# A gated linear-attention layer and its feed-forward layer: all token chunks in pairs of two batches, with the small matrix products on 64x64 parts of the array

## Chip, core and metric

The kernel runs on one core of a Trainium2 chip. The metric is the device time of one execution in microseconds (us). Five engines run their own instruction streams and wait for each other through semaphores: TensorE (PE; its weight loads are listed apart as PEld), VectorE (DVE), ScalarE (ACT), GpSimd (POOL) and SyncE (SP), which here issues nearly all DMA transfers. SBUF is the on-chip memory, PSUM the eight-bank memory that TensorE writes its products to.

## The reference

Four batches, eight heads, 768 tokens, 48 numbers per head. A state of 48x48 per batch and head decays by `w` and takes up one outer product per token; the output `y` of a token reads the state, and its own outer product with a bonus weight `u`. The outputs of the eight heads (384 numbers) then pass through two dense layers with a leaky ReLU between them.

```
for t in range(S):                      # S = 768; r, k, v, w: [4, 8, 768, 48]
    cur = einsum('bhd,bhe->bhde', u * k[t], v[t])
    y[t] = einsum('bhd,bhde->bhe', r[t], state + cur)
    state = w[t][..., None] * state + einsum('bhd,bhe->bhde', k[t], v[t])
x = y.transpose(0, 2, 1, 3).reshape(3072, 384)
h = x @ w_in                            # 384 -> 2048
out = maximum(0.01 * h, h) @ w_out      # 2048 -> 384
```

## The kernel before

**Chunks.** The recurrence is cut into chunks of 128 tokens, 6 per batch, 24 in all (numbered `n` in the order in which they are worked on, `seq`). Inside a chunk, the running sums of log w make decayed copies of r and k, and y comes from three products: masked scores (r times k) with v, the carried state with r, and the bonus. The next state is the decayed state plus k times v. One chunk uses, per engine:

- SP: a load each of w, k, r, v (line 701 for single chunks).
- ACT: log of w (711), the exponentials (743, 747) and the decay of the whole chunk, `a` (738).
- TensorE: running sums of log w by a triangular matrix (717) and the chunk totals against a column of ones (720); transposes of r and k (416); scores (858); new sums for the state, k times v (798); carried state with r (824); masked scores with v (829); transposes of y (464).
- DVE: the exponents' sums (729), products with r and k (405), masks on the scores (788), bonus reduction (443), new state (813), y plus bonus (478).
- POOL: bonus products (435, 439, 447), cast of v (455), decayed state (775).

**Two forms.** `pair` (483 to 685) works on two consecutive chunks of one batch, two tokens to a partition; it serves the first two chunks of batches 0 and 1, n = 0 to 3, with the state handed from the first to the second chunk inside it (592 to 612). Its scores (624) run on 64x64 parts of the array and its masked products (649) and state sums (583) on 64x128 parts; the bonus is added by TensorE (`add_vs`, 668) and y is only copied (678, 680). `single` (687 to 845) works on one chunk, one token to a partition, for n = 4 to 23; in seven cases (`MERGED`) the scores of two singles are issued together by `run`.

**Transposes by DMA.** For the chunks in `RK_DMA` the transposes of r and k, and for those in `Y_DMA` the transposes of y, are made by DMA transfers that SP issues (764, 843); for the others by TensorE.

**Dense layers.** `blocks` of one or two chunks: the first matrix product (901, "up") fills a PSUM bank, ACT applies the leaky ReLU (916), the second product (928, "down") sums over 16 pieces, DVE or ACT copies the result (939, 941), SP stores it (945). Weights are loaded in pieces through the buffers `in` and cast to bf16 (335 to 361).

**Order.** Nothing is ordered by hand: `Plan` (23 to 152) lists all steps with engines, assumed costs, priorities and buffers, runs an event simulation, and the instructions are then issued in the order that this gave, on every engine in order. `RANK` (162) adds offsets to the priorities of the first 144 steps and `FORCE` (179) fixes the engine of some. Each PSUM use takes one of eight banks `ps`, with limits per kind (319). `LEAD` and `AHEAD` say how far log w and the loads may run ahead. Until 24 us, gaps of TensorE in the plan are filled with products of zeros (970).

Of the kernel before, what the change touches and what calls it, by code (L numbers as in the profile page):

```python
# [15 lines left out]
class Buf:  # L16


    def __init__(self, pool, kind=None):
        self.pool, self.kind, self.users, self.t, self.free_at = pool, kind or pool, [], None, 0.0  # L20


class Plan:
# [7 lines left out]
    def __init__(self, limits, slack_from, slack, late):  # L31
        self.steps, self.limits, self.late = [], limits, late
        self.slack_from, self.slack = slack_from, slack
# [8 lines left out]
    def order(self, pools):  # L42
# [10 lines left out]
        remain = {k: len(b.users) for k, b in bufs.items()}  # L53
        free_tiles = {p: [(0.0, k) for k in range(len(t))] for p, t in pools.items()}
        in_use = {}
        ready_at = [0.0] * n
        self.start, self.done, self.eng = [None] * n, [0.0] * n, [None] * n
# [15 lines left out]
        while events:  # L73
# [13 lines left out]
            for e in self.ENGINES:  # L87
# [3 lines left out]
                while ready[e]:  # L91
# [3 lines left out]
                    want, ok = {}, True  # L95
                    for b in self.steps[i][5]:
                        if b.t is None:
                            want[b.pool] = want.get(b.pool, 0) + 1
                            if in_use.get(b.kind, 0) >= self.limits.get(b.kind, 99):
                                ok = False  # L100
                    for p, k in want.items():
                        if sum(f <= now + 1e-9 for f, _ in free_tiles[p]) < k:
                            ok = False
# [10 lines left out]
                for b in takes:  # L114
                    if b.t is None:
                        slots = free_tiles[b.pool]
                        s = min(slots)
                        slots.remove(s)
                        b.slot = s[1]
                        b.t = pools[b.pool][s[1]]  # L120
                        in_use[b.kind] = in_use.get(b.kind, 0) + 1
                d = engs[e]
                self.start[i], self.eng[i] = now, e
# [7 lines left out]
                else:  # L131
# [5 lines left out]
                    self.done[i] = dma_free + lat + (self.late if now > 20 else 0.0)  # L137
                heapq.heappush(events, (free[e], 1, e, -1))
# [5 lines left out]
                for b in {id(b): b for b in (*reads, *takes)}.values():  # L144
                    b.free_at = max(b.free_at, self.done[i])
                    remain[id(b)] -= sum(u == i for u in b.users)
                    if remain[id(b)] == 0:
                        free_tiles[b.pool].append((b.free_at, b.slot))
# [7 lines left out]
BOTH = (1.5, 64, 1.45, 0.2)  # L156
WEIGHT = (2.08, 24, 2.6, 0.2)
# [4 lines left out]
RANK = {0: 15.37, 1: 14.4, 2: 3.33, 3: 23.03, 4: 38.76, 5: 12.01, 6: -26.8, 7: -21.87, 8: -21.96, 9: -19.05,  # L162
# [22 lines left out]
def kernel(  # L185
# [91 lines left out]
    with tc.manual_schedule():  # L277
# [10 lines left out]
        for t in pools["lw"]:  # L288
            nc.vector.memset(t[:, :, D:64], 0.0)
# [715 lines left out]
```

## Time and profile before

| | |
|---|---|
| three runs | 181.78, 182.65, 183.76 us; median 182.65 |
| the profiled execution | 181.38 us, its span 179.6 us |
| granted TensorE clock | 0.996 |
| up products (L901), 720 | 73.3 us busy |
| down products (L928), 384 | 73.4 us busy |
| leaky ReLU (L916, ACT), 96 | 56.8 us busy, 597 ns each |
| masks on single chunks' scores (L788, DVE), 40 | 25.1 us busy, 683 ns each |
| bonus products (L435, L439, POOL), 24 each | 1001 and 1027 ns each |
| loads of single chunks, 80 | 192 KB each, 4.0 to 4.2 us from issue to landing |
| transposes by DMA | 13 of r and k (3.9 us to landing), 8 of y (3.7) |
| moved by DMA | 34.43 MB in 116571 packets, 109121 of them under 512 B |

Times in the profile are counted from the start of the span. A group's busy time merges overlapping instructions of an engine: durations of matrix products overlap, so the distance from one start to the next is what a product takes from TensorE. The chain that ended last follows the work back from the last instruction, each time to what released it. A stretch table gives the busy time of each engine between two times.

### The profile page before, as it was taken

The page shows a single profiled execution, that of the slowest core. Times are in us where ns is not written, and L with a number is a line of the kernel's source. Part 1 is how long each engine was busy: PE and PEld are TensorE (multiplying, and loading weights), DVE is VectorE, ACT ScalarE, POOL GpSimd, SP SyncE. Part 2 cuts the span into 40 slices and gives each one's busy share as a digit, 9 for nine tenths or more (in the row PEclk, how much of TensorE's full clock was granted, in tenths as well). Part 3 has the DMA queues.
Part 4 walks back from the last instruction along what each step waited for, and adds up shares of the span by engine and source line. Part 5 has one row for each costly group of instructions (what it writes and reads, how often), then busy time and mean ns, then how long its engine had stood idle before and what let it go on. Part 6 is the DMA issues. An engine that isn't in the chain of part 4 may idle for free.

```text
span 179.6 us, 5197 instructions
## 1 busy us (share of the span) xinstructions
PE 171.6 (96%) x2036; PEld 129.8 (72%) x2037; DVE 115.0 (64%) x231; ACT 115.3 (64%) x253; POOL 102.5 (57%) x138
## 2 busy tenths in 40 slices
PE   7798999999999999999999999999999999999991
PEld 2466888867778788877788767787788786787850
DVE  7699764289789898559677558397468297241102
ACT  2678968855867788884489774485486664652610
POOL 5999632574897686877469854667165665100000
PEclk9999999999999999999999999999999999999998
DMA  5999999998999999999999989999899996600112
GB/s 141 261 283 316 370 376 364 187 199 199 231 191 224 180 229 134 184 213 173 185 181 223 212 179 223 153 215 175 152 254 170 220 163 134 167 9 19 47 44 88
DMA packets 116571, 34.43 MB, mean 192 GB/s; under 512 B 109121, under 2 KB 115778, under 8 KB 116546
## 3 DMA queue, kind: packets, MB, share of 16 engines
q1 hardware_dynamic: 116544, 34.09, 95.8%
q8 instruction: 16, 0.26, 0.7%
q14 instruction: 9, 0.07, 0.1%
q10 hardware_dynamic: 2, 0.00, 0.0%
HBM read 25.17 MB, written 4.72 MB: 166 GB/s over the span
## 4 chain that ended last, share of the span: by engine, by line
PE 77%; DMA 11%; DVE 4%; ACT 2%; issue 2%; SPq 1%; POOL 0%; DVEq 0%; ACTq 0%
PE ps L901 35%; PE ps L928 28%; DMA in<-in_r_dram 3%; DMA in<-in_v_dram 3%; DMA in<-in_w_dram 2%; PE ps L858 2%; DMA xT<-y 2%; PE ps L829 2%; PE ps L717 2%; PE ps L824 2%; PE ps L416 2%; DVE rk L405 2%; PE ps L798 1%; PE ps L464 1%; DVE m L636 1%
## 5 line engine op out<-in xcount | busy, mean ns | idle before, releaser
L901 PE MATMUL ps<-xT,w_in_b 128*128 128x256 bf16 (+1 forms) x720 | 73.3, 251 | 0.4 <-ACT xT L471 0.2
L928 PE MATMUL ps<-w_out_b,g 128*128 128x384 bf16 x384 | 73.4, 326 | 0.0
L916 ACT ACTIVATE g<-ps 128x512 bf16<-128x512 f32 x96 | 56.8, 597 | 25.4 <-PE ps L901 23.2
L901 PEld LDWEIGHTS <-w_in_b 128*128 128x128 bf16 x720 | 57.8, 98 | 9.9 <-issue 0.7
L928 PEld LDWEIGHTS <-g 128*128 128x128 bf16 x384 | 35.2, 98 | 17.3
L405 DVE TENSOR_TENSOR rk<-in,ps 128x384 bf16<-128x384 f32 x46 | 24.5, 548 | 9.9 <-ACT ps L743 6.5
L435 POOL TENSOR_TENSOR ru<-in,ub 128x384 f32<-128x384 f32 x24 | 23.9, 1001 | 9.6 <-DMA in<-in_k_dram 7.6
L788 DVE TENSOR_TENSOR m<-ps,maskb 128x512 bf16<-128x512 f32 x40 | 25.1, 683 | 5.3 <-PE ps L858 5.3
L439 POOL TENSOR_TENSOR ru<-ru,in 128x384 f32<-128x384 f32 x24 | 24.6, 1027 | 3.0 <-DMA in<-in_r_dram 2.4
L775 POOL TENSOR_TENSOR sb<-s,a 128x384 bf16<-128x384 f32 x18 | 15.0, 831 | 16.8 <-ACT a L738 16.8
L447 POOL TENSOR_TENSOR vs<-in,dg 128x384 f32<-128x384 f32 x20 | 16.6, 830 | 9.1 <-DVE dg L443 8.4
L729 DVE TENSOR_TENSOR ci<-ps,lw 128x384 f32<-128x384 f32 x20 | 11.1, 555 | 9.7 <-PE ps L720 4.5
L939 DVE COPY o<-ps 128x384 f32<-128x384 f32 x10 | 5.6, 555 | 15.6 <-PE ps L928 15.4
L443 DVE TENSOR_REDUCE dg<-ru 128x8 f32<-128x384 f32 x24 | 12.9, 544 | 2.1 <-POOL ru L439 2.1
L478 DVE TENSOR_TENSOR y<-ps,vs 128x384 bf16<-128x384 f32 x20 | 11.1, 553 | 3.2 <-PE ps L829 2.6
L455 POOL CAST vb<-in 128x384 bf16<-128x384 f32 x24 | 12.0, 504 | 1.5 <-DMA in<-in_v_dram 1.4
L711 ACT ACTIVATE lw<-in 128x384 bf16<-128x384 f32 x20 | 10.4, 522 | 2.9 <-DMA in<-in_w_dram 2.9
L743 ACT ACTIVATE ps<-ps 128x384 f32<-128x384 f32 x20 | 9.6, 481 | 4.1 <-DVE ci L729 3.6
L738 ACT ACTIVATE a<-ps 64x4 f32<-64x4 f32 x36 | 6.0, 167 | 7.7 <-DVE ci L729 5.1
L813 DVE TENSOR_TENSOR s<-ps,sb 128x384 f32<-128x384 f32 x14 | 7.7, 552 | 3.8 <-PE ps L798 2.7
L747 ACT ACTIVATE ps<-ci 128x384 f32<-128x384 f32 x20 | 9.8, 491 | 0.0
L941 ACT COPY o<-ps 128x384 f32<-128x384 f32 x14 | 6.7, 479 | 4.2 <-PE ps L928 4.0
(90 smaller groups left out, 176.2 us busy)
## 6 DMA issues: line engine op xcount, KB each, us to landing
out_dram<-o SPq DMA_DIRECT2D x24, 192.0 KB, 3.7
in<-in_w_dram SPq DMA_DIRECT2D x20, 192.0 KB, 4.2
in<-in_k_dram SPq DMA_DIRECT2D x20, 192.0 KB, 4.2
in<-in_r_dram SPq DMA_DIRECT2D x20, 192.0 KB, 4.0
in<-in_v_dram SPq DMA_DIRECT2D x20, 192.0 KB, 4.0
in<-in_moe_w_out_dram SPq DMA_DIRECT2D x4, 768.0 KB, 12.1
in<-in_moe_w_in_dram SPq DMA_DIRECT2D x4, 384.0 KB, 6.8
in<-in_moe_w_in_dram SPq DMA_DIRECT2D x2, 768.0 KB, 9.0
```

Of the source, the lines that this page charges most:

```text
L405: (nc.gpsimd if e == "POOL" else nc.vector).tensor_tensor(out=o, in0=x, in1=i, op=ALU.mult)
L435: lambda e: nc.gpsimd.tensor_tensor(out=ru.t[:], in0=kv(), in1=ubv, op=ALU.mult),
L439: lambda e: nc.gpsimd.tensor_tensor(out=ru.t[:], in0=ru.t[:], in1=rv(), op=ALU.mult),
L443: lambda e: nc.vector.tensor_reduce(out=dg.t[:], in_=ru.t[:], axis=AX.X, op=ALU.add),
L447: lambda e: nc.gpsimd.tensor_tensor(out=vs.t[:], in0=vv(), in1=dg.t[:].unsqueeze(2).to_broadcast([128, H, D]), op=ALU.mult),
L455: {"POOL": 0.56}, lambda e: nc.gpsimd.tensor_copy(out=vb.t[:], in_=vv()),
L478: lambda e: nc.vector.tensor_tensor(out=y.t[:], in0=heads(yp.t), in1=vs.t[:], op=ALU.add),
L775: lambda e: nc.gpsimd.tensor_tensor(out=sb.t[:].rearrange("p g a d -> p (g a) d"), in0=s_in.t[:].rearrange("p g a d -> p (g a) d"), in1=a_ ...
L788: lambda e, par=par: nc.vector.tensor_tensor(out=m.t[:, par, :, :], in0=sc[par].t[:].rearrange("p (g t) -> p g t", g=NP), in1=maskb[:].uns ...
L901: nc.tensor.matmul(hp.t[:, a * N : (a + 1) * N], lhsT=w_in_b[:, t, (j + a) * 128 : (j + a + 1) * 128], rhs=xT[:, t, c0 : c0 + N], start=(a ...
L916: lambda e, hp=hp, g=g, j=j, J=J, N=N: nc.scalar.activation(out=g.t[:, j : j + J, 0:N], in_=hp.t[:, 0 : J * N].rearrange("p (a n) -> p a n ...
L928: nc.tensor.matmul(op.t[:, 0:DM], lhsT=g.t[:, j, off : off + 128], rhs=w_out_b[:, j, :], start=(j == 0), stop=(j == NJ - 1))
```

## The change

Everything works in pairs now, and a pair is the same chunk of two neighbouring batches: batch 0 on partitions 0 to 63, batch 1 on 64 to 127, with two tokens to a partition. `seq` is chunk by chunk over all four batches.

- `pair` (n = 0 and 2) makes the first chunks of batches 0, 1 and 2, 3. There is no state yet, so the chunk totals, the decayed state, its product with r and the identity product that added it are gone. The state sums run on 64x64 parts.
- `late` (n = 4, 6, ... 22) takes the place of `single` and `run`. Running sums come from two products and eight small ones for the totals of both batches. The small products all run on 64x64 parts of the array, with the row part and the PSUM bank tied together, in two steps: scores with half of the carried-state products; then the other half, masked scores with v, and state sums.
- The loads are one transfer per tensor and batch, 64 partitions each, with pieces of 384 bytes in place of 192. `in` is one tile of 33 slots that are taken two or four at a time, where it was ten of four.
- The tokens of a late pair stay in the order (first tokens of all partitions, then second); the leaky ReLU reads its PSUM bank in that order and writes the natural one.
- Transposes by DMA: all pairs from n = 8 on, two chunks per transfer, both for r and k and for y. Before, 13 chunks for r and k and 8 for y.
- The last chunk's down product, copy and store are cut into columns 0 to 255 and 256 to 383.
- `blocks` becomes [2, 2, 1, 1, 2, ...]; `LEAD` 6, `AHEAD` 20; `RANK` and `FORCE` are empty. The plan now takes neighbouring slots, keeps a bank from being used by TensorE and another engine at once, and doubles TensorE's costs before 6.5 us.
- At the start: eight small selects on POOL for a new mask `maskp`, one for `maskb` and three memsets less; on DVE memsets of `u_row` and of two more `rk` tiles.

The core of the diff:

```diff
-RANK = {0: 15.37, 1: 14.4, 2: 3.33, 3: 23.03, 4: 38.76, 5: 12.01, 6: -26.8, 7: -21.87, 8: -21.96, 9: -19.05,
...
-FORCE = {23: "DVE", 26: "DVE", 29: "ACT", 30: "DVE", 46: "ACT", 58: "ACT", 61: "ACT", 79: "ACT", 85: "DVE",
...
+RANK = {}
+FORCE = {}
...
-    RK_DMA = {6, 11, 12, 14, 15, 16, 17, 18, 19, 20, 21, 22, 23}
-    Y_DMA = {8, 10, 16, 17, 20, 21, 22, 23}
-    MERGED = {6, 10, 12, 14, 16, 18, 20}
-    LEAD = 4
-    AHEAD = 4
+    RK_DMA = {8, 10, 12, 14, 16, 18, 20, 22}
+    Y_DMA = {8, 10, 12, 14, 16, 18, 20, 22}
+    LIMITS = {"hp": 2, "op": 2, "cp": 1, "ek": 3, "yy": 2, "warm": 1, "warm2": 1}
+    LAST = [(0, 256), (256, DM)]
+    LEAD = 6
+    AHEAD = 20
-    blocks = [2, 1, 1, 1, 1, 2, 2, 2, 2, 2, 1, 1, 2, 2, 2]
+    blocks = [2, 2, 1, 1, 2, 2, 2, 2, 2, 2, 2, 2, 2]
+    seq = [(b, c) for c in range(C) for b in range(B)]
...
+        def late(n):
...
+                for x in range(2):
+                    def load(e, src=src, name=name, x=x):
+                        nc.sync.dma_start(
+                            out=Flat(slots[name]).t.rearrange("p (h f) -> p h f", h=H)[64 * x : 64 * x + 64],
+                            in_=src[b + x, :, t0 : t0 + L, :].rearrange("h (p j) d -> p h (j d)", j=2))
...
+            def scores(e):
+                for js in range(2):
+                    for g in range(NP):
+                        for par in range(2):
+                            q0 = 64 * par
+                            for x in range(2):
+                                q = slice(64 * x, 64 * x + 64)
+                                nc.tensor.matmul(
+                                    scs[js][par].t[q, g * 128 : (g + 1) * 128].rearrange("p (j t) -> p j t", j=2),
+                                    lhsT=rkT2.t[q0 : q0 + D, js, NP + g, q], rhs=rkT2.t[q0 : q0 + D, :, g, q],
+                                    start=True, stop=True, skip_group_check=True)
+            def sums(e):
+                for g in range(NP):
+                    for js in range(2):
+                        for x in range(len(pps)):
+                            q = slice(64 * x, 64 * x + 64)
+                            for par in range(2):
+                                nc.tensor.matmul(
+                                    pps[x].t[64 * par : 64 * par + 64, g * D : (g + 1) * D],
+                                    lhsT=rk2.t[q, js, 1, 2 * g + par, :], rhs=vbs[js].t[q, 2 * g + par, :],
+                                    start=(g == 0 and js == 0), stop=(js == 1), skip_group_check=True)
+            def inter(flip):
+                def go(e):
+                    for g in range(NP):
+                        for x in range(2):
+                            par = x ^ flip
+                            q0, h = 64 * par, 2 * g + par
+                            for j in range(2):
+                                summed(x, j, slice(h * D, (h + 1) * D), lhsT=rkT2.t[q0 : q0 + D, j, g, 64 * x : 64 * x + 64],
+                                       rhs=sbs[x].t[q0 : q0 + D, g, :])
+                return go
+            def intra(e):
+                for h in range(H):
+                    for js in range(2):
+                        for x in range(2):
+                            q = slice(64 * x, 64 * x + 64)
+                            for j in range(2):
+                                summed(x, j, slice(h * D, (h + 1) * D), lhsT=ms[js].t[q, h % 2, h // 2, 64 * j : 64 * j + 64],
+                                       rhs=vbs[js].t[q, h, :])
...
+            s_sc = step(
+                {"PE": 0.75}, row(inter(1), scores), P0 + 1, deps=[*s_T, *s_sbs], reads=[rkT2, *sbs],
+                takes=[sc for js in range(2) for sc in scs[js]] + yps)
...
+            s_yi = step(
+                {"PE": 0.7 if last else 0.9}, row(inter(0), intra, *([] if last else [sums])), P0 + 2,
+                deps=[*s_ms, *s_vbs, *s_T, *s_sbs, s_rk[1, 0], s_rk[1, 1]], reads=[*ms, *vbs, rk2, rkT2, *sbs],
+                takes=[*yps, *pps])
...
+                def leaky(e, hp=hp, g=g, j=j, J=J, N=N, c0=c0):
+                    o, i = g.t[:, j : j + J, 0:N], hp.t[:, 0 : J * N]
+                    if c0 < B:
+                        i = i.rearrange("p (a n) -> p a n", a=J)
+                    else:
+                        i = i.rearrange("p (a x t) -> p a t x", x=2, t=64) if N == L else i.rearrange("p (s x t) -> p s t x", x=2, t=64)
+                        o = o.rearrange("p a (t x) -> p a t x", x=2) if N == L else o.rearrange("p a (s t x) -> p (a s) t x", x=2, t=64)
+                    nc.scalar.activation(out=o, in_=i, func=AF.Prelu, alpha=0.01)
```

`summed` is a product that adds to `yps[x]` on the partitions of token half `j`; `row` issues its parts one after the other as one step.

More of the change, by code (lines that the diff above doesn't have):

```diff
@@ L753, in single @@
[L753 to L762 removed]
+                        heads(c1.t), lhsT=mat[:], rhs=lw.t[:, j, :, 0:D], start=(j == 0), stop=(j == 1),
@@ new lines, in late @@
+            s_cg = step(
+                {"DVE": 0.55},
+                lambda e: nc.vector.tensor_tensor(out=cg.t[:], in0=heads(c1.t), in1=lw.t[:, 1, :, 0:D], op=ALU.add),
+                P0, deps=[s_cum], reads=[c1, lw], takes=[cg])
+            ek0, ek1, er0 = (Buf("ps", "ek") for _ in range(3))
+            s_k0 = step(
+                {"ACT": 0.5}, lambda e: nc.scalar.activation(out=heads(ek0.t), in_=heads(c1.t), func=AF.Exp, scale=-1.0),
+                P0, deps=[s_cum], reads=[c1], takes=[ek0])
@@ new lines, in late @@
+            s_yi = step(
+                {"PE": 0.7 if last else 0.9}, row(inter(0), intra, *([] if last else [sums])), P0 + 2,
+                deps=[*s_ms, *s_vbs, *s_T, *s_sbs, s_rk[1, 0], s_rk[1, 1]], reads=[*ms, *vbs, rk2, rkT2, *sbs],
+                takes=[*yps, *pps])
+            for x in range(0 if last else 2):
+                sx = Buf("s")
+                prev[b + x] = (sx, [step(
+                    {"DVE": 0.35},
+                    lambda e, x=x, sx=sx: nc.vector.tensor_tensor(
+                        out=sx.t[:], in0=part(pps[x].t), in1=sbs[x].t[:], op=ALU.add),
+                    P0 + 2, deps=[s_yi], reads=[pps[x], sbs[x]], takes=[sx])])
```

875 lines of the change are left out of this document (449 added, 426 removed), and 16 rows, old and new, of the table RANK.

## Prediction

> **What bounds the kernel now.** I read the page first, then busy time by stretch, the chain that ended last, and TensorE's timeline. The page's busy line:
>
> ```profile
> PE 171.6 (96%) x2036; PEld 129.8 (72%) x2037; DVE 115.0 (64%) x231; ACT 115.3 (64%) x253; POOL 102.5 (57%) x138
> DMA  5999999998999999999999989999899996600112
> ```
>
> TensorE leads, but DMA engines read 9 as well, so stretches have to decide (columns: stretch, length, then busy us and count of PE, PEld, DVE, ACT, POOL; clock; DMA share; GB/s):
>
> ```profile
> 19.00:36.00 17.00, 16.77 (x234) 14.15 (x234) 8.61 (x14) 13.38 (x24) 7.99 (x10) 1.00 1.05 321
> 89.00:120.00 31.00, 31.00 (x343) 24.18 (x342) 21.14 (x41) 21.44 (x51) 20.31 (x25) 1.00 1.20 197
> 150.00:176.00 26.00, 25.91 (x221) 18.64 (x220) 6.76 (x13) 10.98 (x20) 2.76 (x4) 1.00 0.24 59
> ```
>
> From 19.0 us (the chain's first L901) to 176.0 TensorE is never without work for more than a few tenths, at full clock. DMA at 1.2 never starves it. So the span is a front of 19.0, 157.0 of TensorE work, and a tail of 3.6 (176.0 to 179.6). Only less TensorE work, an earlier first L901 or a shorter tail can help; any new gap costs in full.
>
> Prices on TensorE come from start-to-start distances, since durations overlap (start, duration, instruction, count):
>
> ```profile
> 60.03 0.33 PE L717 MATMUL ps<-lw,trev 128*128 128x384 bf16 x1
> 60.19 0.24 PE L720 MATMUL ps<-ones,lw 128*128 128x1 bf16 x4
> 60.29 0.33 PE L464 MATMUL ps<-ident,y 128*128 128x128 bf16 x3
> 60.46 0.33 PE L798 MATMUL ps<-vb,rk 128*128 128x96 bf16 x4
> 60.72 0.40 PE L858 MATMUL ps<-rkT 48*128 48x128 bf16 x8
> 61.05 0.82 PE L928 MATMUL ps<-w_out_b,g 128*128 128x384 bf16 x4
> ...
> 64.04 0.33 PE L824 MATMUL ps<-sb,rkT 128*128 128x96 bf16 x4
> 64.21 0.36 PE L829 MATMUL ps<-vb,m 128*128 128x48 bf16 x8
> 64.42 0.61 PE L416 MATMUL ps<-ident,rk 128*128 128x128 bf16 x8
> 64.86 0.33 PE L798 MATMUL ps<-vb,rk 128*128 128x96 bf16 x4
> 65.03 0.33 PE L717 MATMUL ps<-lw,trev 128*128 128x384 bf16 x1
> ```
>
> Decay sums: 0.16 for 384 columns, 0.10 for the four totals. Transposes: y 0.17, r and k 0.44. Sums (L798) 0.17, but 0.26 ahead of L858: 0.09 to enter the split array. Scores of one chunk 0.33; the chain has sixteen of two chunks in 0.55, so eight cost 0.22 and 0.11 is for leaving. A visit to a split array thus costs 0.20 beside its products. Carried state (L824) 0.17, masked product (L829) 0.21.
>
> For small parts there are only the first pairs:
>
> ```profile
> 10.86 0.64 PE L624 MATMUL ps<-rkT 48*64 48x128 bf16 x32
> L624 PE MATMUL ps<-rkT x64: 213/216/240, 10.9 to 18.7; 48*64 48x128 bf16 x64
> L649 PE MATMUL ps<-vb,m x64: 179/179/193, 14.3 to 22.1; 64*128 64x48 bf16 x64
> ```
>
> On four 64x64 parts (L624), 32 products take 0.64 with one duration of 0.216, so (0.64-0.216)/31 = 13.7 ns each: four in 55 ns. L649, on two row parts with 48 columns, runs 32 in 0.57 (14.33 to 14.90): 12.6 each, two in 25 ns. The longest durations are those that waited for a weight load: 240-213 = 27 ns for 64 columns on four parts, 193-179 = 14 on two.
>
> **The change, part by part.** *Late pairs on TensorE (the largest term).* Before, 20 single chunks: decay 20x0.16 + 72/4x0.10 = 5.0; scores 7 merged x(0.55+0.09) + 6 x(0.33+0.09) = 7.0; sums 16x0.17 = 2.7; carried state 18x0.17 = 3.1; masked 20x0.21 = 4.2; transposes on TensorE 7x0.44 + 12x0.17 = 5.1. Sum 27.1. After, ten pairs: decay 0.32+0.20 = 0.52 each, 5.2. First visit: 32 scores x13.7 ns + 16 carried-state products + 0.20; second: 16 + 64 masked + 32 sums (none in the last two pairs) + 0.20. The 48-column product on four parts is nowhere in the trace: between 6.3 ns (four in the 25 ns that a part takes) and 12.6 (four no better than two). I take 7: a part's period is then the 27 ns weight load, which the records show running under the previous product. Visits: 0.75 and 0.98 (0.76 in the last two), so 7.5+9.4 = 16.9. Transposes stay for chunks 4 to 7: 4x(0.44+0.17) = 2.4. Sum 24.5: **-2.6**. There are 1,216 such products, so each ns is 1.2 us: -3.4 to +4.2.
>
> [...]
>
> *Rest of TensorE.* First pair 2 after 19.0 loses the carried-state product and identity add (L656, L601): 4x0.04+0.16, -0.3. Of 288 up-projections with 128 columns, 192 become 96 with 256: 192x0.0556-96x0.109, -0.2. Splitting the last output's columns adds nothing that shows.
>
> *Tail, -0.5.* The last copy is 128 columns for 384: L939's 0.555 less 256 at 1.0 ns (slope from L788: 512 columns 0.683) saves 0.25. The store carries a third; of its 3.0 us (176.56 to the end) I take 0.25.
>
> *Front, -0.5 (bounds -1.5 and +1.0).* First pair 0 loses the state steps that lie between its masks and y (sb 0.47 among them on the chain). Against it: eight more selects on POOL at 0.2 to 0.3 (L306's 0.29 is the nearest), minus one and three memsets, and about 0.8 of DVE memsets; POOL's first bonus product stands at 6.28 directly behind the selects, and `add_vs` needs its results. Loads are the same bytes in two issues each; they wait in SP's queue behind the transfers either way.
>
> *Other engines, nothing.* Per two chunks DVE changes from 9.3 to about 9.0 (state 192 columns), ACT loses about 0.7, POOL gains two half-height products of 0.83 less two halved sb, some +0.8, so 111 of 179. SP: loads 88 to 96, transposes 21 to 16 (double size); late loads move 384-byte pieces, as in the first pairs' slices (261 to 283 GB/s against some 200 later), which covers larger transposes. All lie under TensorE, with 30% free; gone that cover, ACT comes next. The leaky step reads PSUM in alternating halves: no row has that; bounds 0 and the 0.15 by which strided L423 copies differ (0.59 to 0.74); I take 0, off the path.
>
> *New waits, +1.0 (0 to 5).* Pair 4's chunks come as one: w of chunk 4 was issued at 23.5 and TensorE met its y only at 42.4. Twice the loads (1.57 MB, 6 us at 261 GB/s) lie ahead while pairs 0 and 2 last until about 19+21+4: 0.5. The scores take four score banks and two y banks in one step, of eight, and the 144 hand ranks are gone: 0.05 a pair, 0.5. Behind each such wait stand the up and down products, on an engine that runs in order.
>
> Sum: -2.6-0.3-0.2-0.5-0.5+1.0 = -3.1. Span 176.5; with 1.8 around it 178.3 against 181.4. The median of the runs shown is 182.65, so **179.5**.
>
> **Rivals.** *A: four parts do no better than two,* since each part waits for its weights or its instructions. Place: the second visit, 224 instructions with the weight loads against 96 in the densest stretch now (L583 and L649). For it: no 48-column row on four parts, no run so long. Against: the 27 ns. Price 1,216x5.6 ns = +6.8: 186.3, slower. It decides from 9.5 ns a product, where the gain is gone. [...]
>
> *B: TensorE waits in each pair.* Six banks at once need both output kinds nearly drained, and masks hold them for up to 4x0.68. For it: the order is new, and today's has under 1 us of gaps, so it can only get worse. Against: DVE, ACT and POOL are at 57 to 64%. At 0.5 us for ten pairs: 184; at 0.3 no gain is left.
>
> *C: only the cover changes.* The cheaper products are real but the later pair 4 and front eat them (+2.5): 182, no change.
>
> **How the numbers follow.** Forecast 0.48, A 0.18, B 0.19, C 0.15. One per cent, about what a measurement of this kernel can tell, is 180.8 to 184.5. The forecast lies faster in nine cases of ten (0.43), some of C too (0.02); same: the rest of the forecast (0.05), most of C (0.12) and a quarter of B (0.05), 0.22; slower: A, most of B (0.14) and a hundredth of C, 0.33. Range: product at 6.3, front at -1.5 and no waits give 176.6; upper end A's 186.5.
>
> **What would show it.** Right: a 48-column product on 64x64 parts at 7 ns start to start, visits of 0.75 and 1.0, TensorE without gaps from some 18.5 to 172.5. Wrong: 12 ns (A), gaps before scores (B) or before pair 4's first up product (C), or ACT above 600 ns in the leaky step.

## The result: 12% slower, and the profile after

The changed kernel takes 204.63 us (median of four runs, 203.46 to 206.38) against 183.08 for the kernel before (181.78 to 183.76): ratio 1.119, interval [1.108, 1.131]. The forecast was 179.5 with a range up to 186.5: wrong in sign, and outside the range. One run of the experiment with the first pairs' loads at full height, 1.9% above the fastest of its kernel, is left out of its time below.

The changed kernel's profiled execution took 205.48 us, its span 203.8 us. From its page: the busy line, DMA by fortieths of the span, and the queue q8, which brings instructions in packets of 16 KB (packets, MB, share):

```profile
PE 178.5 (88%) x3001; PEld 129.8 (64%) x3004; DVE 111.8 (55%) x234; ACT 103.5 (51%) x201; POOL 115.1 (57%) x165
...
DMA  5999999999999999799999999999999923111112
...
q8 instruction: 23, 0.38, 0.8%
```

TensorE falls from 96% to 88%, with no other engine above 57%, while the DMA engines read 9 nearly throughout, up to the last fifth. The same three stretches as before, changed kernel:

```profile
19.00:36.00 17.00, 15.34 (x203) 11.32 (x204) 9.88 (x17) 9.67 (x18) 7.82 (x10) 0.90 1.10 313
89.00:120.00 31.00, 28.18 (x643) 21.12 (x631) 19.90 (x39) 16.01 (x33) 25.71 (x34) 1.00 1.12 196
150.00:176.00 26.00, 24.41 (x423) 18.17 (x424) 12.47 (x23) 11.17 (x21) 7.44 (x11) 1.00 0.69 117
```

Before, TensorE was busy in all but 0.3 us of these stretches; now it is idle for 1.7, 2.8 and 1.6. What ended its idle time, from the changed kernel's table of waits (line waited, releaser: us, times, longest):

```profile
PE ps L757 <- ACT lw L744: 5.8, 5, 3.3
PE ps L874 <- DMA rkT<-rk: 2.2, 1, 2.2
PE ps L874 <- issue: 2.0, 1, 2.0
...
PE ps L874 <- DVE rk L446: 1.5, 3, 0.8
PE ps L762 <- issue: 1.4, 1, 1.4
...
PE ps L990 <- issue: 1.2, 1, 1.2
...
PE ps L868 <- issue: 0.9, 1, 0.9
```

There are two families. One is late data: running sums (L757) that wait for the log of w (L744), which itself waited for loads of w for 12.9 us, and the carried-state products (L874) that open the step of the scores and wait for a transpose by DMA. The other is "issue", where TensorE waits for nothing that a semaphore shows. One such stop lies inside a second visit to the split array (timeline of TensorE, changed kernel):

```profile
80.88 0.39 PE L874 MATMUL ps<-vb,m 64*64 64x48 bf16 x28
83.27 0.47 PE L874 MATMUL ps<-vb,m 64*64 64x48 bf16 x36 [2.00 <-issue]
83.56 0.44 PE L868 MATMUL ps<-vb,rk 64*64 64x48 bf16 x32
```

Counted in TensorE's instruction stream, the four stops under "issue" after the first up product (5.5 us) fall at numbers 1982, 2238, 3262 and 4286. All leave the rest 190 by 256. The packets of q8 have 16384 bytes, 23 of them for some 6,000 instructions of TensorE, so a packet is taken here as a page of 256 instructions, and each of these stops is at the border of one.

And the front. From 2 to 10 us only the first pairs' loads run, the same bytes in the same 384-byte pieces. The same stretch before, then after (last column GB/s):

```profile
2.00:10.00 8.00, 6.79 (x52) 3.57 (x52) 6.17 (x22) 4.27 (x9) 7.35 (x17) 1.00 1.19 258
```

```profile
2.00:10.00 8.00, 7.28 (x30) 3.46 (x29) 5.73 (x25) 3.86 (x6) 7.35 (x21) 1.00 1.15 199
```

The DMA engines are as busy as before and move a quarter less. In the packet records, a 384-byte piece takes 28.0 ns on average before and 35.2 after. What differs is the transfer: 384 KB to 128 partitions in one, or 192 KB to 64.

The span in four terms, from the starts and ends of matrix products (the row of the forecast is the kernel before with the prediction's terms added; the last three kernels are experiments below):

| us | first up | gaps on TensorE after it | its work after it | tail | span |
|---|---|---|---|---|---|
| before | 19.0 | 0.8 | 156.2 | 3.7 | 179.6 |
| changed | 22.5 | 17.0 | 161.3 | 3.0 | 203.8 |
| forecast | 18.5 | 1.8 | 153.1 | 3.2 | 176.5 |
| first pairs' loads at full height | 19.8 | 15.5 | 161.1 | 3.0 | 199.4 |
| all loads at full height | 19.8 | 3.4 | 157.8 | 3.0 | 184.0 |
| the same, wide masked products | 19.8 | 1.5 | 157.0 | 3.0 | 181.4 |

### The profile page after: what moved, and what is told of

The parts are those of the page before. It is cut to its first block, busy times and chain, and to the rows that moved or that the text cites. A ratio compares the mean times of both kernels' runs of the same rounds, so it can differ in the third digit from the quotient of the medians.

```text
span 203.8 us, 7137 instructions
## 1 busy us (share of the span) xinstructions
PE 178.5 (88%) x3001; PEld 129.8 (64%) x3004; DVE 111.8 (55%) x234; ACT 103.5 (51%) x201; POOL 115.1 (57%) x165
## 4 chain that ended last, share of the span: by engine, by line
PE 41%; DMA 28%; SPq 10%; POOL 9%; issue 5%; DVE 3%; ACT 3%; POOLq 0%; ACTq 0%; DVEq 0%
PE ps L1021 18%; PE ps L990 16%; DMA in<-in_w_dram 12%; DMA in<-in_v_dram 6%; SPq L538 6%; DMA in<-in_r_dram 4%; DMA rkT<-rk 4%; PE ps L874 3%; POOL vs L841 2%; POOL ru L831 2%; SPq L731 2%; DMA out_dram<-o 2%; POOL ru L827 1%; ACT lw L744 1%; PE ps L857 1%
## 5 line engine op out<-in xcount | busy, mean ns | idle before, releaser
L1021 PE MATMUL ps<-w_out_b,g 128*128 128x384 bf16 (+2 forms) x400 | 76.8, 322 | 1.0 <-DVE w_out_b L401 1.0
L841 POOL TENSOR_TENSOR vs<-in,dg 64x384 f32<-64x384 f32 x40 | 33.0, 825 | 3.7 <-DVE dg L835 1.6
L926 DVE TENSOR_TENSOR m<-ps,maskp 128x512 bf16<-128x512 f32 x40 | 24.9, 682 | 11.1 <-PE ps L857 11.1
L827 POOL TENSOR_TENSOR ru<-in,ub 128x384 f32<-128x384 f32 x20 | 19.8, 1000 | 8.4 <-DMA in<-in_k_dram 8.4
L1032 DVE COPY o<-ps 128x384 f32<-128x384 f32 (+1 forms) x14 | 7.5, 537 | 30.1 <-ACT g L1010 18.7
L744 ACT ACTIVATE lw<-in 128x768 bf16<-128x768 f32 x10 | 8.4, 842 | 14.3 <-DMA in<-in_w_dram 12.9
L914 POOL TENSOR_TENSOR sb<-s,a 128x192 bf16<-128x192 f32 x20 | 9.8, 508 | 8.6 <-ACT ps L786 4.7
L835 DVE TENSOR_REDUCE dg<-ru 128x8 f32<-128x384 f32 x20 | 10.8, 548 | 3.3 <-POOL ru L831 3.2
L1066 PE MATMUL ps<-zeros 128*128 128x128 bf16 (+1 forms) x38 | 9.3, 357 | 2.0 <-DVE zeros L319 1.7
L874 PEld LDWEIGHTS <-rkT 48*64 48x64 bf16 x320 | 4.6, 107 | 10.0 <-issue 5.3
L874 PE MATMUL ps<-sb,rkT 48*64 48x48 bf16 x320 | 7.1, 192 | 4.0 <-DMA rkT<-rk 2.2
L1034 ACT COPY o<-ps 128x384 f32<-128x384 f32 (+1 forms) x11 | 5.2, 473 | 9.0 <-PE ps L1021 8.7
L777 DVE TENSOR_TENSOR ci<-ps,lw 128x384 f32<-128x384 f32 x10 | 5.5, 555 | 7.5 <-PE ps L762 2.9
```

The lines of the kernel that those rows point to most:

```text
L827: lambda e, ru=ru, j=j: nc.gpsimd.tensor_tensor(out=ru.t[:], in0=view("k", j)(), in1=ubv, op=ALU.mult),
L835: lambda e, ru=ru, dg=dg: nc.vector.tensor_reduce(out=dg.t[:], in_=ru.t[:], axis=AX.X, op=ALU.add),
L841: lambda e, x=x, j=j, q=q, dg=dg: nc.gpsimd.tensor_tensor(out=vs2[x].t[64 * j : 64 * j + 64], in0=view("v", j)()[q], in1=dg.t[q].unsqueeze ...
L874: nc.tensor.matmul(yps[x].t[64 * j : 64 * j + 64, cols], start=(x, j) not in begun, stop=True, skip_group_check=True, **k)
L926: lambda e, par=par, js=js: nc.vector.tensor_tensor(out=ms[js].t[:, par, :, :], in0=scs[js][par].t[:].rearrange("p (g t) -> p g t", g=NP), ...
L1021: nc.tensor.matmul(op.t[:, d0:d1], lhsT=g.t[:, j, off : off + 128], rhs=w_out_b[:, j, d0:d1], start=(j == 0), stop=(j == NJ - 1))
```

## Experiments

The theory after the result had two parts: loads of half height (to 64 partitions) are slow and make everything behind them late (L), and dense small products run out of instructions (P). Against it stood an order that is worse without its ranks (O), the larger transposes (X), and four parts that are no better than two (A). Ratios are to the kernel before, which was run beside each experiment (medians 181.6 to 181.8 us); the changed kernel was not run again, so differences to its 204.6 us can be off by 1 to 2 us.

**The kernel before with loads of half height.** Every load of r, k, v, w is cut into two of 64 partitions:

```diff
-                    nc.sync.dma_start(out=part(i)(), in_=src[b, :, t0 : t0 + L, :].rearrange("h p d -> p h d"))
+                    for x in (0, 64):
+                        nc.sync.dma_start(
+                            out=part(i)()[x : x + 64], in_=src[b, :, t0 + x : t0 + x + 64, :].rearrange("h p d -> p h d"))
```

(and the first pairs' loads likewise.) 

> The kernel before with every load cut into two transfers of 64 partitions each; same bytes, same pieces, same order. Theory L (transfers of half height are slow, and the changed kernel's late start and its waits for w come from them): between 2 and 10 us the DMA engines move about 200 GB/s in place of 258, the first up product starts at 21 to 23 us in place of 19.0, and the time rises by 4 to 15 us. Theory P (the loss is in the supply of TensorE's instructions) and theory O (the loss is the order without hand ranks): rate, first up product and time stay within 1 us, near 183.

Measured 219.15 us, ratio 1.205 [1.199, 1.211]. From 2 to 10 us it moves 200 GB/s where the kernel before moves 258, and the first up product comes at 24.2: the changed kernel's slow front comes without the rest of the change, and comes out larger (L had 21 to 23). The time, 37 us more, is far beyond L's 4 to 15, for what follows is not a clean copy: 36 to 60 us have only 145 GB/s at a DMA share of 0.72, and the chain has 18.8% of the span in SP issuing the single chunks' loads, which are now twice as many. So this run speaks for the front alone.

**The changed kernel with two queues for the halves.** The second batch's loads of pairs 0 and 2 are issued by ACT.

```diff
-                            nc.sync.dma_start(
+                            (nc.scalar if b else nc.sync).dma_start(
...
-                            {"SP": 0.55}, load, P0 + "wkrv".index(name) * 0.1 + 0.5 * x, takes=[slots[name]],
+                            {"ACT" if b else "SP": 0.55}, load, P0 + "wkrv".index(name) * 0.1 + 0.5 * x, takes=[slots[name]],
```

> The changed kernel with the second batch's loads of the first two pairs (8 of 96 transfers) issued from ScalarE's queue, so that both halves of the partitions are being filled at once. Theory L: 2 to 10 us moves 250 GB/s or more in place of 199, the first up product starts at 19 to 20 in place of 22.5, w of chunk 4 is seen 2 to 4 us earlier, and the time falls by 3 to 7 us to 198 to 201. If the rate is set by the pieces or the memory and not by the height: 199 GB/s again and 204 to 206.

Measured 205.78, ratio 1.132 [1.125, 1.138]; 199 GB/s from 2 to 10 us and the first up product at 22.7, as without the edit, although 4,226 packets (1.57 MB) now come by ACT's queue and alternate with SP's from 4 us on. The queue is not the reason. This is also a miss of L as it was put: L had 250 GB/s or more once both halves are filled at once, and 199 is what the other side foretold. What decides between them are the loads alone and the kernels with loads at full height, below.

**The kernel before without its ranks.**

```diff
-RANK = {0: 15.37, 1: 14.4, 2: 3.33, 3: 23.03, 4: 38.76, 5: 12.01, 6: -26.8, 7: -21.87, 8: -21.96, 9: -19.05,
...
+RANK = {}
+FORCE = {}
```

> The kernel before with empty rank and engine tables, nothing else. Theory O: 8 us or more slower than before, with gaps on TensorE of several us. Theories L and P: at most 3 us slower, TensorE's gaps after the first up product under 3 us in all.

Measured 182.97, ratio 1.006 [1.004, 1.009]: the hand-made order was worth 1.1 us in the kernel before, far from 22.

**Small products alone.** A long run of 48-column products on four 64x64 parts, then bursts of 112 between full products.

```diff
+        burst(768)
+        full(24)
+        for _ in range(6):
+            burst(112)
+            full(24)
```

> Only TensorE products (none of the computation): 768 products of 48 columns on four 64x64 parts in one run, then six bursts of 112 between 24 products of 256 columns on the full array, then twelve such bursts while 64 loads of half height run. Theory P (instructions come in pages of 256, and a dense burst outruns the next page): in the long run 6.3 to 7.5 ns a product inside a page and a stop of 0.5 to 2 us at nearly every 256th instruction; in the bursts without loads fewer or shorter stops, with loads stops of 1 to 2 us at page borders that fall in or shortly behind a burst. If the supply is a steady rate: one even distance between products, above 7 ns, with no stop at any border.

The long run (timeline of TensorE):

```profile
14.31 1.62 PE L32 MATMUL small<-a 64*64 64x48 bf16 x175
18.33 1.23 PE L32 MATMUL small<-a 64*64 64x48 bf16 x128 [2.40 <-issue]
21.79 1.91 PE L32 MATMUL small<-a 64*64 64x48 bf16 x128 [2.23 <-issue]
25.24 1.91 PE L32 MATMUL small<-a 64*64 64x48 bf16 x128 [1.55 <-issue]
```

128 products with their 128 weight loads are 256 instructions, one page. At full clock (the second line) they take 1.04 us, start to start of the first and last, 8.2 ns a product; then TensorE stops until the next page has come, and pages arrive every 3.45 us. No load runs in this stretch (5 GB/s from 18.3 to 33.3 us), so the supply alone is the limit: 13.5 ns an instruction when sustained. The six bursts with full products between them have two such stops (0.4 and 0.7 us); with half-height loads running, the same bursts stop at nearly every border, 0.3 to 1.8 us each. (From some 20 us on, in the midst of the stops, the clock is 0.5; the mean from 18.3 to 33.3 us is 0.56.)

**Loads alone, by shape.** Eight stretches of loads, each begun after the one before has landed; the first two, in which `whole` is a transfer to 128 partitions and `half` one to 64:

```diff
+        for i in range(8):
+            whole(i, i)
+        between()
+        for i in range(16):
+            half(i // 2, 8 + i // 2, i % 2, i % 2)
+        between()
```

> Leaves out all of the computation: only loads, in eight stretches of some 3.1 MB, each begun after the one before has landed (the seventh has 1.6 MB). 1: 8 transfers of 128 partitions, 8 heads, 384-byte pieces. 2: 16 transfers of 64 partitions, lower and upper half in turn. 3: 16 transfers of 64 partitions, lower half alone. 4: 16 transfers of 128 partitions, 4 heads each, so as large as those of 2. 5: 16 transfers of 128 partitions with 192-byte pieces. 6: as 2, lower halves from SP's queue and upper ones from ACT's. 7: 32 transfers of one head for both batches (128 partitions, 384-byte pieces, 49 KB), from two queues. 8: as 1. Theory L (a transfer that reaches only 64 partitions is slow by its height, whatever the number, the size or the queue of the transfers): 1, 4 and 8 reach 250 to 290 GB/s; 2 and 6 stay at some 200, and 3 at 200 or less. Rival S (small transfers are slow, by their size or number): 4 falls to 200 as 2 does, and 7 far below. Rival H (halves are filled one after the other, one half at a time): 6 returns to 250 or more, 3 is slower than 2. Stretch 5 gives the price of the 192-byte pieces that the kernel before used later on: some 200 by the rates of the later stretches there, if those were bound by transfers at all.

The middles of the eight stretches (last two columns: DMA share, GB/s):

```profile
6.00:12.00 6.00, 5.24 (x8) 0.00 (x0) 1.00 1.17 325
24.00:34.00 10.00, 1.52 (x6) 0.00 (x0) 1.00 1.21 223
43.00:53.00 10.00, 2.54 (x10) 0.00 (x0) 1.00 1.32 207
60.00:68.00 8.00, 1.52 (x6) 0.00 (x0) 1.00 1.07 290
77.00:87.00 10.00, 1.52 (x6) 0.00 (x0) 1.00 1.15 222
97.00:105.00 8.00, 1.41 (x6) 0.00 (x0) 1.00 1.28 246
120.00:150.00 30.00, 0.51 (x2) 0.00 (x0) 1.00 0.15 40
159.00:165.00 6.00, 1.27 (x5) 0.00 (x0) 1.00 1.17 325
```

Full height reaches 325 in the first and the last stretch. Half height, halves in turn: 223; lower half alone: 207; halves from two queues: 246. Full height in transfers as small as the halves: 290, so the size and number of the changed kernel's transfers account for a small part at most. 192-byte pieces at full height: 222, what 384-byte pieces reach at half height, so the doubled pieces of the change gained nothing. Over the whole stretches the packet records have 22.3, 30.9, 36.2, 23.1, 15.7 and 30.2 ns a piece in 1 to 6. Stretch 7 is slow as S has it (40 GB/s), but at a DMA share of 0.15, with pieces of 22.1 ns: there the engines mostly stand idle, which is a different limit from the changed kernel's. Theory L holds for transfers of 192 KB, at higher rates than it gave; S falls for them; H gets a little: filling both halves at once gives 8 to 19%, not the 40 to 57% that are missing.

**Masked products on 64x128 parts.**

```diff
-                            for j in range(2):
-                                summed(x, j, slice(h * D, (h + 1) * D), lhsT=ms[js].t[q, h % 2, h // 2, 64 * j : 64 * j + 64],
-                                       rhs=vbs[js].t[q, h, :])
+                            nc.tensor.matmul(
+                                yps[x].t[:, h * D : (h + 1) * D], lhsT=ms[js].t[q, h % 2, h // 2, :], rhs=vbs[js].t[q, h, :],
+                                start=False, stop=True, skip_group_check=True)
```

> The masked products of the later pairs write 128 rows at once: 32 products on 64x128 parts in place of 64 on 64x64 parts, 64 TensorE instructions fewer in each of ten pairs, 2.5 pages of 256 in all. Theory P (TensorE stops about 1.4 us at each 256th instruction where the instructions come closely, because the next 16 KB page of them is fetched only then): the idle time under 'issue' falls from 5.7 us to 3 to 5, the masked products of a pair still take 0.4 to 0.6 us, and the kernel is 0.5 to 3 us faster than the changed kernel (202 to 204). Rival A (four parts at once are what makes the late products quick): the masked products grow from 0.5 to about 1.0 us, five us in all, and the kernel is 3 to 5 us slower (207 to 210), with the same stops.

Measured 202.61, ratio 1.116 [1.112, 1.119] to the kernel before, 2 us less than the changed kernel, though the intervals of the two ratios overlap. Idle time under "issue" after the first up product falls from 5.5 us to 1.1, more than P asked for, but waits for data grow into part of the place (gaps 15.3 in all, against 17.0). One pair's carried-state products, masked products and sums, on four parts in the changed kernel and then with wide masked products (timelines):

```profile
93.20 0.31 PE L874 MATMUL ps<-sb,rkT 48*64 48x48 bf16 x16
93.35 0.68 PE L874 MATMUL ps<-vb,m 64*64 64x48 bf16 x64
93.85 0.60 PE L868 MATMUL ps<-vb,rk 64*64 64x48 bf16 x32
```

```profile
92.22 0.31 PE L874 MATMUL ps<-sb,rkT 48*64 48x48 bf16 x16
92.46 0.57 PE L894 MATMUL ps<-vb,m 64*128 64x48 bf16 x32
92.97 0.44 PE L868 MATMUL ps<-vb,rk 64*64 64x48 bf16 x32
```

From the first masked product to the first sum it is 0.50 us and 0.51, but the two are made up differently. In this pair the narrow products start 7.9 ns apart (8.3 to 8.7 in most others); the wide ones start 12.7 ns apart in every pair, and going from one shape of parts to the other costs 0.1 us each time: the last carried-state product is followed after 118 ns by the first wide one, and the last wide one after 109 ns by the first sum, where it is 22 and 13 ns without a change of shape. So A's cost did not come, but neither do four parts bring anything over two: inside a row two narrow products take 16 ns, one wide product 12.7.

**Transposes through TensorE.**

```diff
-    RK_DMA = {8, 10, 12, 14, 16, 18, 20, 22}
-    Y_DMA = {8, 10, 12, 14, 16, 18, 20, 22}
+    RK_DMA = set()
+    Y_DMA = set()
```

> The late pairs' transposes go through TensorE rather than through the DMA engines: the DMA engines lose the 256-byte transposed packets, TensorE gains some 10 us of work over the kernel. Theory L (the first pairs' loads of half height make the kernel late, and the late pairs' loads wait behind them): the first product (line 990) stays at 22 to 23 us and the wait for the Ln of pair 4 stays at 3 us or shrinks a little, as no transpose runs by then; the rest grows by TensorE's work: 208 to 216 us. Rival X (the transposes crowd the loads out of the DMA engines): loads of 60 to 150 us become faster than 220 GB/s, the waits for lw, rkT and xT vanish (4 to 5 us), and the time is 203 to 208.

Measured 205.78, ratio 1.133 [1.127, 1.139]: about the time of the changed kernel, inside X's 203 to 208 and below L's 208 to 216, although TensorE does 10.8 us more in transposes (L457 and L507, start to start). Gaps fall from 17.0 to 10.7. Loads run at 224 and 221 GB/s from 60 to 84 and 84 to 120 us (202 and 198 in the changed kernel), and the waits for rkT and xT are gone, as X has it; the waits for lw (4.5 us, 2.8 of it before pair 4) stay, as L has it. So the transposes do crowd the loads, but taking them away does not bring the time back.

**Loads at full height inside the changed kernel.** Each tensor of a pair still comes in two transfers of 192 KB with 384-byte pieces; each now brings four heads of 256 tokens of one batch to 128 partitions. The tokens are then not those that a pair's products need, so these kernels tell of the time alone and are no way to make the layer. First for the first two pairs only:

```diff
-                                out=Flat(slots[name]).t.rearrange("p (h f) -> p h f", h=H)[64 * b : 64 * b + 64, h0:h1, :],
-                                in_=src[b0 + b, h0:h1, 0:L, :].rearrange("h (p j) d -> p h (j d)", j=2))
+                                out=Flat(slots[name]).t.rearrange("p (h f) -> p h f", h=H)[:, 4 * b : 4 * b + 4, :],
+                                in_=src[b0, 4 * b : 4 * b + 4, 0 : 2 * L, :].rearrange("h (p j) d -> p h (j d)", j=2))
```

> The loads of the first two pairs alone get full height: the two transfers of a tensor bring four heads each of 256 tokens of one batch to 128 partitions, in place of eight heads of 128 tokens of one batch to 64 partitions. Number, size (192 KB), pieces (384 bytes) and all waits stay; the tokens are others than the pair should work on. Theory L (the height of the first loads makes the kernel late, 22 ns a piece at full height against 30 to 35 at half): 2 to 10 us move 250 to 290 GB/s in place of 199, the first up product (line 990) comes at 18.5 to 20 in place of 22.5, the 3.3 us before line 757 for pair 4's Ln fall to 0 to 2, the half clock from 40.6 us goes with them; the stops without a semaphore stay at some 5: 195 to 199 us. Rival R (the front is late by its own work, the masks on POOL and the order of the plan): rates rise, but the first up product stays after 21.5, and the time is above 201.

Measured 199.4 (199.2 to 201.2), ratio 1.099 [1.095, 1.104]. The front behaves as L says: 263 GB/s, first up product at 19.8. But the span is only 4.4 us shorter, less than L's 5 to 9. Pair 4's running sums still wait 2.7 us, where L had 0 to 2: they wait for the log of pair 4's own w, whose loads this edit leaves at half height. Rival R falls.

Then for the late pairs too:

```diff
-                            out=Flat(slots[name]).t.rearrange("p (h f) -> p h f", h=H)[64 * x : 64 * x + 64],
-                            in_=src[b + x, :, t0 : t0 + L, :].rearrange("h (p j) d -> p h (j d)", j=2))
+                            out=Flat(slots[name]).t.rearrange("p (h f) -> p h f", h=H)[:, 4 * x : 4 * x + 4, :],
+                            in_=src[b + c % 2, 4 * x : 4 * x + 4, c // 2 * 2 * L : (c // 2 + 1) * 2 * L, :].rearrange(
+                                "h (p j) d -> p h (j d)", j=2))
```

> As the run before, with the late pairs' loads too at full height (four heads of 256 tokens of one of the two batches, in each transfer); each byte of the inputs is still loaded once. Theory L: besides, the later waits for Ln (lw, 2.5 us) and part of those for transposes by DMA (rkT, xT, 2.6) go, 2 to 5 us more: 191 to 197. Rival X (the later waits are of the transposes' and the pages' making, whatever the loads): within 1 us of the run before.

Measured 186.32, ratio 1.025 [1.021, 1.029]: 13 us less than the run before, far past the 2 to 5 that L was given. The waits of TensorE that are left:

```profile
PE ps L869 <- issue: 0.8, 2, 0.6
...
PE ps L875 <- DVE rk L446: 0.7, 3, 0.4
PE ps L875 <- DMA rkT<-rk: 0.7, 1, 0.7
PE ps L763 <- issue: 0.4, 1, 0.4
...
PE ps L758 <- ACT lw L745: 0.2, 1, 0.2
```

Waits for lw are 0.2 us where they were 5.8, and the stops at page borders are 1.4 where they were 5.5, with the same instructions. Between 36 and 120 us a 384-byte piece takes 24 to 26 ns instead of 31 to 37, and TensorE has no gap from 36 to 60 (stretches 36 to 60 and 84 to 120 us, this kernel):

```profile
36.00:60.00 24.00, 24.00 (x550) 18.46 (x548) 20.44 (x42) 17.44 (x38) 22.69 (x30) 1.00 1.06 256
...
84.00:120.00 36.00, 34.06 (x711) 25.45 (x709) 23.27 (x47) 20.42 (x42) 27.37 (x37) 1.00 1.11 224
```

Nothing but the loads was changed, so the two families of stops have one root for the most part, the half-height loads. For the waits for data the way is plain. For the pages, the records show when they were fetched: in the changed kernel the transfer of a page that came late began 2.3 to 4.3 us after TensorE had begun the page before, took 0.9 to 1.4 us, and TensorE went on 1.3 to 1.7 us after it had landed. In the long run of small products without loads the transfers began after 1.0 to 1.2 us. Rival X falls.

And with wide masked products besides (the edit shown above): 

> As the run before, with the masked products on 64x128 parts besides (64 TensorE instructions fewer in a late pair). If the stops at pages are a cost of their own: 1 to 3 us faster than the run before. If they cost only because slow loads hold the page's transfer up: the same within 0.5 us. No theory has it below the kernel before (181.65) by more than 1 us, since the late products' work saved nothing that can be seen (24.4 us against 21.5 without transposes).

Measured 183.45, ratio 1.008 [1.006, 1.011], 2.9 us faster than the run before it. The table of waits has nothing under "issue" after the first up product any more, and TensorE's own work falls by 0.8. The stops at page borders so cost something of their own, 1.4 us of the 2.6 by which the span is shorter, once the loads are out of the way.

**One part of the change alone in the kernel before: the last output in two pieces of columns.**

```diff
-                op = Buf("ps", "op")
+                for d0, d1 in ([(0, 256), (256, DM)] if ch == NCH - 1 else [(0, DM)]):
+                    op = Buf("ps", "op")
...
-                                op.t[:, 0:DM], lhsT=g.t[:, j, off : off + 128], rhs=w_out_b[:, j, :],
+                                    op.t[:, d0:d1], lhsT=g.t[:, j, off : off + 128], rhs=w_out_b[:, j, d0:d1],
```

> The kernel before with one part of the change alone: the last chunk's down product, copy and store cut into columns 0 to 255 and 256 to 383. The tail of the changed kernel is 3.1 us against 3.6, so 0.5 us faster, ratio 0.997; if the shorter tail came from elsewhere, 1.000.

Measured 181.0 against 181.79, ratio 0.996 [0.994, 0.9975]; the tail is 3.2 us for 3.7. This is the only version here that beats the kernel before, by 0.4%.

**Which 64 partitions.** Loads alone again, always 64 partitions in a transfer:

```diff
+        for rows in (slice(0, 64), slice(32, 96), slice(0, 128, 2), slice(64, 128), slice(32, 96)):
+            for i in range(16):
+                part(i, 8 + i // 2, i % 2, rows)
+            between()
```

> Leaves out all of the computation: only loads, in seven stretches of 3.1 MB with 384-byte pieces, each begun after the one before has landed. 1 and 7: 8 transfers to 128 partitions. 2 to 6: 16 transfers to 64 partitions each: partitions 0 to 63; 32 to 95; every second one of 0 to 127; 64 to 127; 32 to 95 again. [...] Rival N (it counts how many partitions a transfer reaches): all of 2 to 6 at 200 to 220 GB/s. [...]

The middles of the seven stretches:

```profile
6.00:12.00 6.00, 5.23 (x8) 0.00 (x0) 1.00 1.17 325
24.00:36.00 12.00, 3.00 (x12) 0.00 (x0) 1.00 1.29 194
42.00:51.00 9.00, 3.29 (x13) 0.00 (x0) 1.00 1.07 281
57.00:66.00 9.00, 3.23 (x13) 0.00 (x0) 1.00 1.02 271
72.00:84.00 12.00, 3.02 (x12) 0.00 (x0) 1.00 1.31 197
91.00:100.00 9.00, 2.84 (x12) 0.00 (x0) 1.00 0.96 252
105.00:112.00 7.00, 1.49 (x6) 0.00 (x0) 1.00 1.17 324
```

Partitions 0 to 63 get 194 GB/s, 64 to 127 get 197; 32 to 95 get 281 and 252, every second one 271. Over the whole stretches the pieces take 38.0, 37.6, 23.3 and 23.1, and 23.1 ns. Stretches 2 to 6 load the same data. So it is not how many partitions a transfer reaches but which: rival N, with 200 to 220 GB/s for all of 2 to 6, falls. Why one half by itself is slow, no run here shows.

## Why the prediction was wrong

**The step that failed** is "Other engines, nothing", where it says that late loads move 384-byte pieces "as in the first pairs' slices (261 to 283 GB/s against some 200 later), which covers larger transposes". The rate was read from transfers to 128 partitions and carried over to transfers to 64 of one half, a shape that no row before had; by the prediction's own rule it should have had two bounds. In the front, "Loads are the same bytes in two issues each" made the same mistake. In DMA engine time: the loads before took 81,920 pieces at 18.8 ns and 8,192 at 28.0, over 16 engines 110 us; after, 49,152 at 35.2, 108 us. What fewer pieces saved was eaten nearly in full. The transposes rose from 16,384 pieces at 25.8 ns (26 us) to 22,528 at 33.7 (47 us), in DMA engines that already read 9 in the kernel before. "DMA at 1.2 never starves it" was true of that kernel alone.

What it cost, by the runs at full height: of the 24.2 us by which the span grew, 19.8 go with the height of the loads alone: 2.7 of front, 13.6 of gaps, and 3.5 of TensorE's work. Part of this last is the clock, which the records of the changed kernel put at 0.5 from 20.1 to 23.5 and from 40.6 to 44.0 us, the second soon after the 3.3 us wait (twelve up products take 2.40 us at 40.3 and 1.49 at 83.9); how the rest divides was not tried.

**New waits, +1.0 (0 to 5):** 16.2, the term in which the loss shows; 2.7 with all loads at full height. Pair 4 was named as the place with 0.5; it took 3.3, since its w, issued at 21 and 24, was not in ACT's hands before 38.2. The order was put at 0.5; removing the ranks before costs 1.1.

**Late pairs on TensorE, -2.6.** This step failed too, by a smaller sum, and here the mechanism was right and the size wrong. Counted from each product's start to the next, without the gaps, the late pairs' work at full height is 28.1 us (24.5 counted), and that of the single chunks before 27.6 (27.1 counted): 0.5 more instead of 2.6 less. What a visit costs was right: a split product behind a full one costs 94 ns at full height and 96 in the kernel before (0.09 counted), and leaving takes 0.11 to 0.14 (0.11 counted). The product was mis-sized. The 1,216 small products start 8.5 ns apart on the average, not 7, which is 1.8 us: a part takes 34 ns a product, where 27 had been read from two durations. Another 1.5 us stand where a wait or a page border falls among them, since the last product before it counts with its whole 0.19 to 0.21 us; the decay sums are 0.3 over. TensorE's work as a whole is 157.8 us against 156.2: 1.6 more instead of 3.1 less.

**Rest of TensorE:** up products of 128 and 256 columns take 56 and 109 ns start to start, as counted; against that, the products of zeros that fill gaps before 24 us took 1.0 us more at full height than before. **Tail, -0.5:** 0.7, and 0.4% by itself in the kernel before. **Front, -0.5 (to +1.0):** +3.5; at full height +0.8, inside the bounds.

**Rivals.** A had two halves. That four parts do no better than two is borne out: inside a row two narrow products take 16 ns, one wide product 12.7. But its price of 12.6 ns for a narrow product is not: 8.5. That TensorE waits for instructions in the second visit is shown, but as stops at some borders of 256 instructions and not as a price of each: inside a page of the small products alone it is 4.06 ns an instruction, and the 13.5 ns of the long run are set by its pages. At four borders of the changed kernel the stops came to 5.5 us. B, a wait for banks in each pair, was not seen in the changed kernel: the table of waits names data or pages, not a bank that is still being read. C, cover gone at pair 4 and in the front, named two of the right places with 2.5 us; they took 3.3 and 3.5, and most of the new gaps lay elsewhere.

**Open:** what sets the start of a page's transfer, which takes 1.1 to 1.2 us on the average in the kernel before, the changed one and the one at full height; what TensorE waits for between a page's landing and its next instruction; and how large the loss is in a kernel that loads at full height, or to partitions of both halves, and still computes the layer, for none was built. Even with the loads' loss taken out the changed kernel stays 2.5% behind the kernel before, and 0.8% with wide masked products.

## What to carry to other kernels

Price a load by the partitions that it reaches, not by bytes and piece length alone: with 384-byte pieces, partitions 0 to 63 or 64 to 127 alone ran at 194 to 207 GB/s, the two in turn at 223 (246 from two queues), where 32 to 95, every second one, or all 128 ran at 252 to 325. When a change re-cuts loads, their rate is a term of the sum with its own bounds, even where another engine sets the end; 30% of room on the other engines was no cover against a quarter less from DMA engines that had no room themselves. And splitting matrix products finer adds instructions (64 masked products in a pair where 32 wide ones do): where the narrow form is no faster than the wide one (16 ns for two, 12.7 for one), take the wide one, since TensorE stopped at borders of 256 instructions (5.5 us in the changed kernel, 1.4 with all loads at full height), but count 0.1 us for each change of shape (118 and 109 ns here).

## What the runs showed that was not expected

- In the runs of loads alone, a 384-byte piece takes 22 to 23 ns where a transfer reaches both halves of SBUF (partitions 0 to 63 and 64 to 127) and 36 to 38 where it reaches one; 30 to 31 when transfers to both halves are in flight.
- Instructions come 256 at a time, every 3.45 us in the long run of small products, where TensorE runs through a page in 1.04 us. The stop is 0.3 to 2.4 us, and no semaphore shows it; in the changed kernel the stops came to 5.5 us, with full-height loads to 1.4.
- Transfers of one head for two batches (49 KB, full height, from two queues) reach only 40 GB/s, 2.5 us for each on its queue, at a DMA share of 0.15.
- Going from 64x64 to 64x128 parts of the array, or back, costs 0.1 us (118 and 109 ns from the last product of one shape to the first of the other, against 22 and 13 without a change).
